# State products of units 2 and 3 in four 64x64 tiles, with two steps of the opening moved

## The chip, the cores and the metric

The kernel runs on one core of a Trainium2 chip. The metric is the device time of one execution in microseconds, as the median of several runs. All times below are microseconds unless marked ns. The engines are TensorE (in the profile PE for its matmuls, PEld for its weight loads), VectorE (DVE), ScalarE (ACT), GpSimd (POOL) and SyncE (SP, which issues DMAs).

## The reference

A retention layer is followed by a feed-forward layer with a leaky ReLU whose slope differs by channel:

```python
for t in range(S):                       # q, k, v: 4 batches, 8 heads, 768 tokens, 64
    state = gamma * state + outer(k[t], v[t])      # gamma differs by head
    y[t] = scale * q[t] @ state
x = y.transpose(0, 2, 1, 3).reshape(3072, 512)
h = x @ w_in                             # 512 x 2048
g = maximum(h, 0) + alpha * minimum(h, 0)
out = g @ w_out                          # 2048 x 512, float32
```

## The kernel before, in words

**Tiling.** The 3072 tokens are 12 units of 256 (three units to a batch), and two units make a block of 512 for the feed-forward layer, six blocks in all. Inside a unit there are two chunks c of 128 tokens. The recurrence is computed by chunks: within a chunk as masked scores times v, and across chunks as the query times a 64x64 state per head, which is carried from chunk to chunk with a decay of gamma^128. Units 2 and 5 are the last of their batches; unit 3 begins a batch, so that it has a state for its second chunk only.

**Steps of a unit.** `rescale` multiplies k and q by powers of gamma, `turn_pe` transposes them on TensorE and ScalarE copies the result to `kq`, `score_mm` and `masks` make the masked scores, `sum_mm` makes the chunk sums of k times v. `state_sum` adds the carried state to a chunk's sum on VectorE (line 423) and multiplies by the decay (line 424, on the engine that the call names, V for VectorE and G for GpSimd). `state_copy` (lines 428 to 452) writes the float16 copy from which TensorE reads. `out_mm` (lines 492 to 543) makes y: state products first, then scores times v (line 533). `take_y` turns y into xT, the input of the feed-forward layer.

**Two layouts of the state.** Heads go in pairs p; a is the head's place in its pair. For units below SPLIT = 4 the states of a pair stand block-diagonally in a 128x128 tile (`tg`), and one matmul multiplies both heads' queries (line 501): four per chunk. For units from 4 on they stand as 64x64 tiles (`th`), with chunk c's states on partition half c, so that the four products of a pair (two chunks, two heads) use the four 64x64 quarters of the array (line 515): eight per chunk. Queries of head a stand on partition half a of `kq`. Where a differs from c, `move_q` (lines 207 to 220) copies them to the other half, in tile `qf`, and `state_copy` writes the half of the states that changes its partitions ("far") on ScalarE.

**Feed-forward.** `ffn1` is x times w_in with the leaky ReLU (ScalarE, then VectorE), `ffn2` the product with w_out for block 0; the later blocks use a seven-product scheme. w_out's 2048 rows are 16 groups of 128, called ft. Groups 0 to 7 are loaded early in float32 (`get_wo32`) and cast by GpSimd and VectorE (`cast_wo`, two groups a call). Groups 8 to 11 and 12 to 15 come by `get_wo(2)` and `get_wo(3)`, DMAs on GpSimd's queue that cast on the way (line 982).

**What sets the order.** The order on every engine is written out by hand: each engine works in the order in which the calls stand in the code. `ffn1` and `ffn2` are generators that stop after each matmul, and `tick(gen, m)` runs m more of them at that place. `ffn2(0, ..., parts=4)` (lines 800 to 824) goes through its 64 matmuls in this order: for each four of the ft, for each of four token quarters, those four ft. Between its ticks stand units 2 and 3's steps and the ticks of `half`, the first product of block 1. `held.append(get_wo(2))` makes the next query load on SyncE's queue wait for that DMA (`hold`, line 129).

**The opening.** Units 0 and 1 are prepared while w_in arrives in parts; each part is cast by GpSimd or ScalarE (`cast_wi`, lines 974 to 978). The first seven matmuls of block 0's first product read parts 0 and 1 and stand ahead of unit 1's output.

Of the kernel before, what the change touches and what calls it, by code (L numbers as in the profile page):

```python
# [22 lines left out]
def kernel(  # L23
# [20 lines left out]

    SPLIT = 4
    MID = 6
    U = 256
# [90 lines left out]
    def rows(x):  # L140
        return slice(64 * x, 64 * x + 64)
# [53 lines left out]
    def cast_v(eng, u, h0=0, h1=H):  # L195
        o = unit(u)[2][:, h0:h1].rearrange("p h r d -> p (h r d)")
        i = staged[u]["v"][:, h0:h1].rearrange("p h x -> p (h x)")
        if eng is nc.scalar:
            eng.activation(out=o, in_=i, func=COPY, bias=0.0, scale=1.0)
        else:  # L200
            eng.tensor_copy(out=o, in_=i)  # L201
# [2 lines left out]
        kdq, kq, _ = unit(u)  # L204
        nc.sync.dma_start_transpose(out=kq, in_=kdq.rearrange("p t r h d -> p (t r h d)"))

    def move_q(u, eng=None):

        _, kq, _ = unit(u)
        qf = sbp.tile([128, 2, NP, 64], F16, tag="qf", bufs=3, name=f"qf{u}")  # L210
        moved[u] = qf
        for c in range(2):
            o = qf[rows(c)]
            i = kq.rearrange("p (t r a) i -> p t r a i", t=2, r=2)[
                rows(1 - c), 1, :, :, rows(c)
            ]
            if eng is not None:
                eng.activation(out=o, in_=i, func=COPY, bias=0.0, scale=1.0)
            else:
                nc.sync.dma_start(out=o, in_=i)  # L220

    def turn_pe(u, hh, bank):

        kdq, kq, _ = unit(u)
        trb = ps(bank, "trb", F16, 1024)
        n = 0
        for t in range(2):
            for r in range(2):
                for p in (2 * hh, 2 * hh + 1):
                    nc.tensor.transpose(  # L230
                        out=trb[:, n : n + 128],
                        in_=kdq[:, t, r, 2 * p : 2 * p + 2, :].rearrange("p a d -> p (a d)"),
                        identity=ident,
                    )
                    n += 128
        nc.scalar.activation(  # L236
            out=kq.rearrange("p (x a) i -> p x a i", x=4)[:, :, 2 * hh : 2 * hh + 2, :],
            in_=trb.rearrange("p (x a i) -> p x a i", x=4, a=2),
            func=COPY,
            bias=0.0,  # L240
            scale=1.0,
        )
# [167 lines left out]
    def state(u, c, eng, copy="gg"):  # L410

        state_copy(state_sum(u, c, eng), copy)
# [15 lines left out]
    def state_copy(uct, copy="gg", part=None):  # L428

        if uct is None:  # L430
            return
        u, c, t = uct
        to = (u, 1) if c == 0 else (u + 1, 0)
        if to[0] >= SPLIT:
            tg = tgs.get(to) or tgs.get((to[0], 1 - to[1]))
            if tg is None:
                tg = sbp.tile([128, 2, NP, 64], F16, tag="th", bufs=3, name=f"th{to[0]}")
        else:
            tg = tgbuf[(2 * u + c) % len(tgbuf)]
        tgs[to] = tg  # L440
        for a in range(2):
            if copy[a] == "-":
                continue
            far = to[0] >= SPLIT and a != to[1]
            if part is not None and far != part:
                continue
            i = t[rows(a)]
            o = tg[rows(to[1]), a] if to[0] >= SPLIT else tg[rows(a), :, rows(a)]
            if far or copy[a] == "a":
                nc.scalar.activation(out=o, in_=i, func=COPY, bias=0.0, scale=1.0)  # L450
            else:
                nc.gpsimd.tensor_copy(out=o, in_=i)
# [39 lines left out]
    def out_mm(u, banks, evict=True):  # L492
        _, kq, vx = prepped[u]
        ys = [ps(banks[0], "y0"), ps(banks[1], "y1")]
        inter = [(u, c) in tgs for c in range(2)]
        assert inter == [u % UPB > 0, True]

        for c in range(2):
            for p in range(NP):
                if inter[c] and u < SPLIT:  # L500
                    nc.tensor.matmul(
                        out=ys[c][:, 128 * p : 128 * p + 128],
                        lhsT=tgs[u, c][:, p, :],
                        rhs=kq.rearrange("p (t r a) i -> p t r a i", t=2, r=2)[
                            :, 1, :, p, rows(c)
                        ],
                        start=(p == 0),
                        stop=False,
                        skip_group_check=True,
                    )  # L510
        for p in range(NP):
            for c in range(2):
                for a in range(2):
                    if inter[c] and u >= SPLIT:
                        nc.tensor.matmul(  # L515
                            out=ys[c][rows(a), 128 * p : 128 * p + 128],
                            lhsT=tgs[u, c][rows(c), a, p, :],
                            rhs=qmove(kq, a, c, p) if a == c else moved[u][rows(c), :, p, :],
                            start=(p == 0),
                            stop=False,  # L520
                            skip_group_check=True,
                        )
        for p in range(NP):
            m2s = live[u, p // 2]
            for r in range(2):
                for c in range(2):
                    for a in range(2):
                        o = ys[c][rows(a), 128 * p : 128 * p + 128]
                        at, n = 256 * r + 128 * (p % 2), 128
                        if u >= SPLIT and r == 1:  # L530
                            at, n = 256 + 64 * (p % 2), 64
                            o = o.rearrange("p (r i) -> p r i", r=2)[:, :, 32:64]
                        nc.tensor.matmul(  # L533
                            out=o,
                            lhsT=vx[rows(c), 2 * p + a, r, :],
                            rhs=m2s[a][rows(c), at : at + n],
                            start=(r == 0 and p == 0 and not inter[c]),
                            stop=(r == 1),
                            skip_group_check=True,
                        )  # L540
        live[u] = ys
        if evict:
            take_y(u, (0, 1))
# [20 lines left out]
    def w_sums(i, lo, hi, eng=nc.vector):  # L564

        w = w_out_all.rearrange("p (k f) (j e) -> p k f j e", k=2, j=2)
        w12, w21, w22 = w[:, 0, lo:hi, 1, :], w[:, 1, lo:hi, 0, :], w[:, 1, lo:hi, 1, :]
        t1, t2, t3, t4 = (wsum[:, x, lo:hi, :] for x in range(4))
        o, a, b = (
            (t1, w12, w[:, 0, lo:hi, 0, :]), (t2, w22, t1), (t3, w22, w12), (t4, w21, t2)  # L570
        )[i]
        return eng.tensor_tensor(out=o, in0=a, in1=b, op=SUB)  # L572
# [386 lines left out]
    def tick(gen, m=10**6):  # L959
        for _ in range(m):  # L960
            if next(gen, 1) == 1:
                return
# [11 lines left out]
    def cast_wi(eng, lo, hi):  # L974
        o, i = w_in_all[:, :, 128 * lo : 128 * hi], win_part(lo, hi)
        if eng is nc.scalar:
            return eng.activation(out=o, in_=i, func=COPY, bias=0.0, scale=1.0)
        return eng.tensor_copy(out=o, in_=i)  # L978
# [18 lines left out]
    V, G, A = nc.vector, nc.gpsimd, nc.scalar  # L997
# [63 lines left out]
    take_y(0, (1,), V)  # L1061
    cast_v(G, 1, 0, 4)
    cast_v(G, 1, 4, 8)
    state_copy(s01, "g-")
    cast_wi(G, 0, 1)
    score_mm(1, 0, (4, 5))
    masks(1, 0)
    turn_pe(1, 1, 1)
# [1 line left out]
    cast_wi(A, 1, 2)  # L1070
    keep(2, 0)
    sum_mm(1, (6, 7))
    state(1, 0, V, "ga")
    cast_wi(G, 2, 3)
    cast_wi(A, 3, 4)
    get_wi(12, 14)
# [7 lines left out]
    s11 = state_sum(1, 1, V)  # L1084
    gen = ffn1(0, (2, 3, 6, 7, 0, 1, 2, 3, 6, 7, 4, 5, 0, 1, 2, 3), apart=4)
    tick(gen, 7)
    cast_wi(G, 4, 6)
    cast_wi(G, 6, 8)
    state_copy(s11)
    get_wo32(2)  # L1090
    get_wo32(3)
    load(2, "v")
# [18 lines left out]

    gen = ffn2(0, (0, 1, 2, 3), parts=4)
    half = ffn1(1, (6, 7, 4, 5, 4, 6, 0, 1, 2, 3, 0, 4, 5, 6, 7, 1), apart=12)
    tick(gen, 8)
    turn_pe(2, 0, 5)
    tick(gen, 6)
# [2 lines left out]
    masks(2, 0)  # L1119
    wsum = sbp.tile([128, 4, HF, HM], F16, tag="wsum", name="wsum")  # L1120
    turn_pe(2, 1, 4)
    tick(gen, 5)
    score_mm(2, 1, (6, 7))
    sum_mm(2, (5, 4))
    state(2, 0, G, "ga")
    masks(2, 1)
    held.append(get_wo(2))
    load(4)
# [3 lines left out]
    get_wo(3)  # L1132
    cast_v(G, 3)
    w_sums(0, 0, HF, G)
    tick(gen, 7)
    out_mm(2, (4, 5))
    tick(gen, 6)
    tick(half, 24)
    turn_pe(3, 0, 6)
    tick(half, 8)  # L1140
    turn_pe(3, 1, 7)
    tick(half, 16)
    tick(gen, 9)
    score_mm(3, 0, (4, 5))
    masks(3, 0)
    sum_mm(3, (6, 7))
    state(3, 0, G, "ga")
    rescale(G, 4, 0, 0, 8)
    tick(gen, 8)
    score_mm(3, 1, (4, 5))  # L1150
# [25 lines left out]
    a, b = steps(6, 3, 5, 0, "p"), steps(4, 6, 2, 1, "v")  # L1176
# [11 lines left out]
    for n in range(1, NBLK):  # L1188
        more = n + 1 < NBLK
        u0 = 2 * (n + 1)  # L1190
        if n > 1:
            gen = begun
# [22 lines left out]
        if more and u0 >= MID:  # L1215
# [34 lines left out]
            s11 = behind_middle(m11)  # L1250
# [87 lines left out]
```

## Time and profile before

| | us |
|---|---|
| median of 3 runs (198.47 to 198.94) | 198.59 |
| the profiled execution, its own time | 198.86 |
| its span, first to last instruction | 196.9 |
| TensorE's matmuls busy | 189.3 (96%) |
| VectorE / ScalarE / GpSimd busy | 156.3 / 115.4 / 106.1 |

The profile is of one execution. A row of the timeline has the start and the length in microseconds, the engine, the line of the kernel, the operation, output tile <- inputs, shapes, and how many instructions of that kind are merged in it (x8); in brackets stands the idle time of the engine before them and what ended it. Matmuls are pipelined, so that the length of a merged row runs beyond the start of the next; what a step costs TensorE is read from start to start. A row of the stretches has, for each engine, its busy time and number of instructions, then the granted TensorE clock, the share of the DMA engines and GB/s.

### The profile page before, as it was taken

The page shows a single profiled execution, that of the slowest core. Times are in us where ns is not written, and L with a number is a line of the kernel's source. Part 1 is how long each engine was busy: PE and PEld are TensorE (multiplying, and loading weights), DVE is VectorE, ACT ScalarE, POOL GpSimd, SP SyncE. Part 2 cuts the span into 40 slices and gives each one's busy share as a digit, 9 for nine tenths or more (in the row PEclk, how much of TensorE's full clock was granted, in tenths as well). Part 3 has the DMA queues.
Part 4 walks back from the last instruction along what each step waited for, and adds up shares of the span by engine and source line. Part 5 has one row for each costly group of instructions (what it writes and reads, how often), then busy time and mean ns, then how long its engine had stood idle before and what let it go on. Part 6 is the DMA issues. An engine that isn't in the chain of part 4 may idle for free.

```text
span 196.9 us, 6085 instructions
## 1 busy us (share of the span) xinstructions
PE 189.3 (96%) x2529; PEld 128.8 (65%) x2529; DVE 156.3 (79%) x259; ACT 115.4 (59%) x199; POOL 106.1 (54%) x113
## 2 busy tenths in 40 slices
PE   6688999999999999999999999999999999999993
PEld 2356645568467688744688744788644788865882
DVE  7698987517698998289988389977489996999983
ACT  4458665349187668467467476467466486678110
POOL 3176897499549544970077980076970180039300
PEclk9999999999999999999999999999999999999998
DMA  5999999998879989898988899929865010400014
GB/s 156 313 317 380 374 381 377 293 180 136 211 192 200 286 197 265 213 311 175 213 203 209 256 201 191 222 65 225 256 122 126 17 57 3 160 3 0 0 65 152
DMA packets 90026, 37.92 MB, mean 193 GB/s; under 512 B 57984, under 2 KB 87696, under 8 KB 90000
## 3 DMA queue, kind: packets, MB, share of 16 engines
q1 hardware_dynamic: 88768, 36.45, 69.2%
q0 software_dynamic: 1056, 1.05, 3.6%
q8 instruction: 20, 0.33, 0.6%
q10 hardware_dynamic: 176, 0.04, 0.1%
q14 instruction: 6, 0.05, 0.1%
HBM read 27.31 MB, written 6.29 MB: 171 GB/s over the span
## 4 chain that ended last, share of the span: by engine, by line
PE 90%; SPq 4%; DMA 3%; DVE 0%; issue 0%; POOL 0%; DVEq 0%
PE hps L632 36%; PE ox L857 16%; PE oy L857 12%; PE ops L809 7%; SPq L165 4%; PE hps L719 4%; PE sp L761 3%; DMA vs<-in_v_dram 3%; PE y L533 1%; PE y L384 1%; PE trb L230 1%; PE st L284 1%; PE sca L466 1%; PE ov L857 1%; PE ow L857 1%; PE oz L857 1%
## 5 line engine op out<-in xcount | busy, mean ns | idle before, releaser
L632 PE MATMUL hps<-xT,win 128*128 128x512 f16 (+1 forms) x396 | 71.5, 338 | 0.3 <-DVE ss L423 0.3
L650 DVE SCALAR_TENSOR_TENSOR gt<-hm,oma,hps 128x512 f16<-128x512 f32 (+1 forms) x96 | 59.4, 656 | 12.1 <-issue 4.3
L648 ACT ACTIVATE hm<-hps 128x512 f32<-128x512 f32 x80 | 47.6, 597 | 24.6 <-PE hps L632 22.5
L632 PEld LDWEIGHTS <-win 128*128 128x128 f16 x396 | 38.1, 98 | 31.0 <-POOL win L978 0.4
L857 PEld LDWEIGHTS <-gs 128*128 128x128 f16 x320 | 31.0, 98 | 3.7
L857 PEld LDWEIGHTS <-gt 128*128 128x128 f16 x240 | 22.9, 98 | 4.0
L333 POOL CAST tg<-tm 64x256 f16<-64x256 f32 x12 | 4.8, 396 | 34.3 <-DVE tm L301 22.3
L185 POOL TENSOR_TENSOR kdq<-qs,tab 128x1024 f16<-128x1024 f32 (+1 forms) x12 | 20.2, 1686 | 3.0 <-DVE wsum L572 2.3
L185 POOL TENSOR_TENSOR kdq<-ks,tab 128x1024 f16<-128x1024 f32 (+1 forms) x12 | 20.2, 1686 | 2.6 <-PE y L515 2.6
L857 PE MATMUL ox<-wout,gt 128*128 128x256 f16 x144 | 17.3, 273 | 0.0
L857 PE MATMUL oy<-wsum,gs 128*128 128x256 f16 x144 | 17.2, 273 | 0.0
L556 ACT ACTIVATE xT<-y 128x512 f16<-128x512 f32 x22 | 14.9, 744 | 3.1 <-PE y L533 2.0
L201 POOL CAST vx<-vs 128x1024 f16<-128x1024 f32 (+1 forms) x13 | 12.6, 970 | 6.7 <-DMA vs<-in_v_dram 6.7
L809 PE MATMUL ops<-wout,gt 128*128 128x512 f16 x64 | 15.3, 380 | 0.0
L613 DVE TENSOR_TENSOR gs<-gt 128x1024 f16<-128x1024 f16 (+1 forms) x14 | 13.0, 934 | 0.2
L877 ACT ACTIVATE cu<-oy 128x512 f32<-128x512 f32 x10 | 6.0, 597 | 10.6 <-PE oy L857 10.1
L236 ACT ACTIVATE kq<-trb 128x1024 f16<-128x1024 f16 x8 | 8.2, 1023 | 6.3 <-PE trb L230 6.3
L313 POOL TENSOR_TENSOR tf<-ss,tab 128x256 f32<-128x256 f32 x10 | 10.3, 1028 | 2.5 <-DVE ss L312 1.3
L881 DVE TENSOR_TENSOR os<-ox,cu 128x512 f32<-128x512 f32 x5 | 3.4, 687 | 10.1 <-PE ox L857 10.1
L670 POOL TENSOR_SCALAR hn<-qc,oma 128x256 f32<-128x256 f32 x4 | 4.5, 1138 | 12.4 <-DVE qc L785 12.3
L809 PEld LDWEIGHTS <-gt 128*128 128x128 f16 x64 | 5.8, 98 | 6.0
L424 POOL TENSOR_TENSOR tf<-ss,tab 128x256 f32<-128x256 f32 x6 | 5.9, 980 | 7.1 <-DVE ss L423 7.1
(119 smaller groups left out, 293.1 us busy)
## 6 DMA issues: line engine op xcount, KB each, us to landing
qs<-in_q_dram SPq DMA_DIRECT2D x9, 512.0 KB, 5.4
ks<-in_k_dram SPq DMA_DIRECT2D x32, 128.0 KB, 3.5
vs<-in_v_dram SPq DMA_DIRECT2D x32, 128.0 KB, 4.6
early<-in_moe_w_in_dram SPq DMA_DIRECT2D x7, 512.0 KB, 7.5
out_dram<-os SPq DMA_DIRECT2D x9, 256.0 KB, 2.5
early<-in_moe_w_out_dram SPq DMA_DIRECT2D x4, 512.0 KB, 7.0
out_dram<-ot SPq DMA_DIRECT2D x4, 512.0 KB, 3.8
ks<-in_k_dram SPq DMA_DIRECT2D x6, 256.0 KB, 6.1
```

Of the source, the lines that this page charges most:

```text
L165: nc.sync.dma_start(out=t[nm[0]][:, h, :], in_=src[b, h, U * c : U * c + U, :].rearrange("h (p r) d -> p h (r d)", r=2),)
L185: return eng.tensor_tensor(out=kdq[:, t, :, h0:h1, :].rearrange("p r h d -> p h r d"), in0=staged[u]["kq"[t]][:, h0:h1, :].rearrange("p h ...
L201: eng.tensor_copy(out=o, in_=i)
L236: nc.scalar.activation(out=kq.rearrange("p (x a) i -> p x a i", x=4)[:, :, 2 * hh : 2 * hh + 2, :], in_=trb.rearrange("p (x a i) -> p x a ...
L313: nc.gpsimd.tensor_tensor(out=t, in0=ss, in1=dec, op=MULT)
L556: nc.scalar.activation(out=o, in_=i, func=COPY, bias=0.0, scale=1.0,)
L613: last_g.append(nc.vector.tensor_tensor(out=o, in0=a, in1=b, op=op))
L632: nc.tensor.matmul(out=hps[:, f, U * (ul - lo) : U * (uh - lo)].rearrange("p (u t) -> p u t", t=U), lhsT=w_in_all[:, hp, 128 * (f0 + f) : ...
L648: nc.scalar.activation(out=hm, in_=hps, func=RELU, bias=0.0, scale=-1.0)
L650: nc.vector.scalar_tensor_tensor(out=gt[:, f0 + f, U * lo : U * hi], in0=hm[:, f, :], scalar=oma_sb[:, f0 + f : f0 + f + 1], in1=hps[:, f, :],
L809: nc.tensor.matmul(out=opss[tq], lhsT=gt[:, ft, 128 * tq : 128 * tq + 128], rhs=w_out_all[:, ft, :], start=(ft == 0), stop=(ft == NFT - 1),)
L857: nc.tensor.matmul(out=o[1][m], lhsT=lhs(f, m), rhs=rhs(f), start=(first and f == 0 and (m == 0 or o[0] is None)), stop=(f == HF - 1), ski ...
```

## The change

A new limit `QUARTERS = 2` takes the place of `SPLIT` in `state_copy` and `out_mm`, so that units 2 and 3 also use the 64x64 tiles; their other steps keep the layout of before. Their queries are moved by ScalarE, for unit 3 those of the second chunk alone. The state that unit 1 hands to unit 2 is copied in two steps, the near half at the old place and the far half after block 0's first product. Around unit 2's output the ticks of `gen` are 8 and 7 instead of 7 and 6, and a later tick is 8 instead of 9. In the opening, the cast of w_in's part 0 goes ahead of a state copy on GpSimd, and the decay of unit 1's first state goes from VectorE to GpSimd.

```diff
+    QUARTERS = 2
     SPLIT = 4
...
-    def move_q(u, eng=None):
+    def move_q(u, eng=None, cs=(0, 1)):
...
-        for c in range(2):
+        for c in cs:
...
-        if to[0] >= SPLIT:
+        if to[0] >= QUARTERS:
...
-            far = to[0] >= SPLIT and a != to[1]
+            far = to[0] >= QUARTERS and a != to[1]
...
-            o = tg[rows(to[1]), a] if to[0] >= SPLIT else tg[rows(a), :, rows(a)]
+            o = tg[rows(to[1]), a] if to[0] >= QUARTERS else tg[rows(a), :, rows(a)]
...
-                if inter[c] and u < SPLIT:
+                if inter[c] and u < QUARTERS:
...
-                    if inter[c] and u >= SPLIT:
+                    if inter[c] and u >= QUARTERS:
...
+    cast_wi(G, 0, 1)
     state_copy(s01, "g-")
-    cast_wi(G, 0, 1)
     score_mm(1, 0, (4, 5))
...
-    state(1, 0, V, "ga")
+    state(1, 0, G, "ga")
...
-    state_copy(s11)
+    state_copy(s11, part=False)
...
     half = ffn1(1, (6, 7, 4, 5, 4, 6, 0, 1, 2, 3, 0, 4, 5, 6, 7, 1), apart=12)
+    state_copy(s11, part=True)
     tick(gen, 8)
...
     turn_pe(2, 1, 4)
+    move_q(2, A)
     tick(gen, 5)
...
-    state(2, 0, G, "ga")
+    state(2, 0, G)
     masks(2, 1)
     held.append(get_wo(2))
...
     w_sums(0, 0, HF, G)
+    tick(gen, 8)
+    out_mm(2, (4, 5))
     tick(gen, 7)
-    out_mm(2, (4, 5))
-    tick(gen, 6)
     tick(half, 24)
...
     tick(half, 16)
-    tick(gen, 9)
+    move_q(3, A, (1,))
+    tick(gen, 8)
     score_mm(3, 0, (4, 5))
     masks(3, 0)
     sum_mm(3, (6, 7))
-    state(3, 0, G, "ga")
+    state(3, 0, G)
```

## The prediction

> **What bounds the kernel now.** First the page: busy shares and the chain of waits.
>
> ```profile
> span 196.9 us, 6085 instructions
> PE 189.3 (96%) x2529; PEld 128.8 (65%) x2529; DVE 156.3 (79%) x259; ACT 115.4 (59%) x199; POOL 106.1 (54%) x113
> PE 90%; SPq 4%; DMA 3%; DVE 0%; issue 0%; POOL 0%; DVEq 0%
> ```
>
> TensorE is busy 96% of the span and carries 90% of the chain that ended last. After the opening the chain holds next to nothing else. So two things count: how long TensorE's instructions take, and any moment at which it stands still; nothing later has room to give a standstill back. Next I read TensorE's timeline around the touched units, because its matmul counts show how far the interleaved second product of block 0 (line 809, `gen`) has come at each point.
>
> ```profile
> 31.68 1.89 PE L809 MATMUL ops<-wout,gt 128*128 128x512 f16 x8
> ...
> 33.85 1.46 PE L809 MATMUL ops<-wout,gt 128*128 128x512 f16 x6
> ...
> 36.04 1.24 PE L809 MATMUL ops<-wout,gt 128*128 128x512 f16 x5
> ...
> 37.92 1.68 PE L809 MATMUL ops<-wout,gt 128*128 128x512 f16 x7
> 39.44 0.74 PE L501 MATMUL y<-kq,tg 128*128 128x128 f16 x8
> 40.11 0.64 PE L533 MATMUL y<-m,vx 64*64 64x128 f16 x32
> 40.68 1.47 PE L809 MATMUL ops<-wout,gt 128*128 128x512 f16 x6
> ...
> 48.46 2.11 PE L809 MATMUL ops<-wout,gt 128*128 128x512 f16 x9
> ...
> 55.17 0.38 PE L501 MATMUL y<-kq,tg 128*128 128x128 f16 x4
> ...
> 56.06 1.68 PE L809 MATMUL ops<-wout,gt 128*128 128x512 f16 x7
> ```
>
> The counts are the ticks: 8, 6, 5, 7, then unit 2's output (L501, L533), then 6. That is 32 by 42 us, and the 33rd comes only at 48.46. The generator with parts=4 runs four row groups of w_out (ft) for each of four token quarters, so every 16 matmuls it moves on by four groups. Exactly 32 use ft 0 to 7; the 33rd is the first to read ft 8. Those rows do not come by the early loads but by `get_wo(2)`, a DMA that GpSimd issues. So the third view is GpSimd's timeline, with what SyncE's queue waits for.
>
> ```profile
> 38.59 0.61 POOL L424 TENSOR_TENSOR tf<-ss,tab 128x256 f32<-128x256 f32 x1 [2.15 <-DVE ss L423]
> 39.27 0.39 POOL L452 CAST tg<-tf 64x256 f16<-64x256 f32 x1
> 39.61 0.99 POOL L982 DMA_DIRECT2D wout<-in_moe_w_out_dram  x1
> ```
> ```profile
> SPq L165 <- DMA wout<-in_moe_w_out_dram: 6.8, 1, 6.8
> ```
> ```profile
> 46.50 0.38 SPq L165 DMA_DIRECT2D qs<-in_q_dram  x1
> ```
> ```profile
> DMA to landing us min/median/max: 5.5/6.2/6.8
> ```
>
> `get_wo(2)` is issued at 39.61, behind the state's decay and copy of unit 2. The query load of unit 4 is made to wait for it (`hold`), waits 6.8 us and goes at 46.50. So ft 8 to 11 land at about 39.61 + 6.8 = 46.4. Before, TensorE needs them at 48.46, two microseconds later, and nobody notices.
>
> **The change, part by part.** *The moved ticks.* The diff makes 7 and 6 around unit 2's output into 8 and 7. Together with 8, 6 and 5 that is 34, so matmuls 33 and 34, which read ft 8 and 9, now stand ahead of the 24 `half` matmuls. (The tick of 9 becoming 8 brings the count to 42 again at the same later place.) When does TensorE get there? One L809 matmul costs (2.11 - 1.24)/4 = 0.217. From 37.92: eight are 1.74, unit 2's output is 0.91 (next part), five more are 1.09: 37.92 + 1.74 + 0.91 + 1.09 = 41.66. The data are there at 46.4. TensorE waits 46.4 - 41.65 = 4.75 us, and everything behind matmul 33 in its queue waits with it: the `half` matmuls, unit 3's transposes, and through them ScalarE's and VectorE's ReLU work. The issue cannot be earlier: GpSimd works in order, the decay ahead of it waits for VectorE's sum, which waits for TensorE's own products, and the diff leaves one near copy there as before. Any shift of the opening moves both ends alike. The nearest bound from below is the quicker landing of the two, 5.5 after issue, at 45.1: 3.45. I take 4.75, as its row is the same transfer at the same moment.
>
> *The clock behind such a stop.* Inside the span TensorE never stops that long, so the price is bounded by its two ends.
>
> ```profile
> 1.51 3.79 PE L106 MATMUL kps<-spin 128*128 128x512 f16 x10 [1.51 <-DVE spin L1004]
> ```
> ```profile
> 193.70:195.60 1.90, 0.00 (x0) 0.00 (x0) 0.41 (x1) 0.00 (x0) 0.00 (x0) 1.00 0.72 251
> 195.70:196.90 1.20, 0.00 (x0) 0.00 (x0) 0.00 (x0) 0.00 (x0) 0.00 (x0) 0.50 0.00 0
> ```
>
> In the table by stretches the column before the last two is the granted clock. After the last matmul it is still 1.00 until 195.6, and 0.50 from 195.7: less than two microseconds of rest halve it. The first row shows the way back: ten 512-wide matmuls on a rested TensorE take 3.79, where 10 x 0.217 and 0.16 for the last one's drain (2.11 - 9 x 0.217) would be 2.33. So one recovery costs 1.46. Bounds are 0 (the clock stays) and 2.9 (two such stretches until it rises). I take 1.46.
>
> *The four tiles of unit 2.* Eight matmuls of 128x128 become sixteen of 64x64, four of which (chunk c, head half a) work side by side. Units 4 and 5 already do this; unit 5 has the same neighbours, a 128-row product on either side:
>
> ```profile
> 75.49 1.91 PE L857 MATMUL oy<-wsum,gs 128*128 128x256 f16 x16
> ...
> 77.58 0.52 PE L533 MATMUL y<-m,vx 64*64 64x128 f16 x32
> ```
> ```profile
> 77.33 0.26 PEld L515 LDWEIGHTS <-th 64*64 64x64 f16 x16 [0.21 <-issue]
> ```
> ```profile
> L515 PEld LDWEIGHTS <-th x32: 102/106/107, 73.6 to 77.5; 64*64 64x64 f16 x32
> ```
>
> Sixteen 256-wide matmuls at half of 0.217 end their streaming at 77.24; the tiles start at 77.33, 0.09 later, and the next step at 77.58, so sixteen cost 0.25. Unit 2's L533 with its way out takes 40.68 - 40.11 = 0.57 and stays. New: 0.09 + 0.25 + 0.57 = 0.91. Old: 40.68 - 39.44 = 1.24, in which the second half of L501 also waited for the copy that ends at 39.66; one tick later it no longer does. Gain 0.33.
>
> The sixteen loads of unit 5 take 0.26 together, at 0.106 for one of them. [...]
>
> *Unit 3.* It has a state for the second chunk only: four matmuls become eight, and these use one half of the array rows, two side by side, so four rounds as in unit 5. Old: 56.06 - 55.17 = 0.89; new 0.09 + 0.25 + 0.57 = 0.91; +0.02, or down to -0.1 if the next product fills the idle half.
>
> *Queries and states on ScalarE.*
>
> ```profile
> L218 ACT ACTIVATE qf<-kq x4: 615/628/629, 68.7 to 73.2; 64x512 f16<-64x512 f16 x4
> ```
> ```profile
> 39.24 0.41 ACT L450 ACTIVATE tg<-tf 64x256 f16<-64x256 f32 x1 [1.97 <-POOL tf L424]
> ```
>
> Two query moves are 1.25 us behind unit 2's second transpose copy; ScalarE idles 1.97 before 39.24, so it is done by 38.6. Unit 3's one move and the far half of unit 1's last state (0.41) lie likewise in idle time, and its near half alone stays on GpSimd. Cost 0; without that cover the two moves would delay unit 2's output by up to 1.25, but the wait for ft 8 would swallow it.
>
> *The opening.*
>
> ```profile
> 15.72 0.61 POOL L978 CAST win<-early 128x512 f16<-128x512 f32 x1
> 16.86 0.39 POOL L452 CAST tg<-tf 64x256 f16<-64x256 f32 x1 [0.52 <-DVE tf L424]
> ```
> ```profile
> 16.16 0.63 ACT L977 ACTIVATE win<-early 128x512 f16<-128x512 f32 x1
> ```
> ```profile
> 16.37 0.42 DVE L424 TENSOR_TENSOR tf<-ss,tab 128x256 f32<-128x256 f32 x1
> ...
> 18.77 0.73 DVE L554 CAST xT<-y 128x512 f16<-128x512 f32 x1
> ```
> ```profile
> 16.39 0.96 PE L632 MATMUL hps<-xT,win 128*128 128x256 f16 x7 [0.29 <-DVE ss L423]
> 17.18 0.61 PE L501 MATMUL y<-kq,tg 128*128 128x128 f16 x8
> 17.72 0.74 PE L533 MATMUL y<-m,vx 64*64 64x128 f16 x32
> ```
> ```profile
> 18.39 0.88 PEld L632 LDWEIGHTS <-win 128*128 128x128 f16 x9
> 19.55 2.51 PEld L632 LDWEIGHTS <-win 128*128 128x128 f16 x21 [0.29 <-DVE xT L554]
> ```
> ```profile
> L424 POOL TENSOR_TENSOR tf<-ss,tab x6: 612/832/1529, 12.6 to 73.4; 128x256 f32<-128x256 f32 x6
> ```
>
> The cast of w_in part 0 ends at 16.33 and the seven matmuls start at 16.39. Moved ahead of a copy of 0.39, it ends some 0.3 earlier. But the fifth of the seven reads part 1, which ScalarE casts until 16.79, and now starts at 16.39 + 4 x 0.109 = 16.83. So the seven end where they do: 0. The decay leaves VectorE (0.42) for GpSimd, behind cast and copy, at about 16.45. GpSimd's six decays took 0.61 to 1.53. I take 0.61 (the row at 38.59, with mask products on VectorE as here): ready at 17.1, copied by 17.5, where the second half of L501 would start at 17.4. A wait of about 0.15. In return the masks come 0.4 earlier and the stall of L533 for them (0.67 for 17.72 to 18.39, where unit 2 needs 0.57) goes: 18.45 instead of 18.39. Behind it nine matmuls (0.98) run before xT is needed; now xT ends at 19.50, just after them, then at about 19.35. TensorE goes on at 19.45 instead of 19.55: -0.1, from -0.2 up to +0.8 with the decay at 1.53.
>
> **Sum.** -0.1 - 0.33 + 0.02 + 4.75 + 1.46 = +5.8. The profiled execution took 198.86 (its span 196.9 and 2.0 around it), 0.27 above the median of 198.59. So 198.86 + 5.8 = 204.66, and for the median 204.4.
>
> **The rivals.** *The rows are there in time.* If ft 8 had landed by 41.65 there would be no stop and no loss of clock: 198.59 - 0.41 = 198.2, no measurable change. It decides at a landing 2.0 us after issue; the shortest in the trace is 5.5, and nothing ahead of it on GpSimd gets shorter. 5%.
>
> *The clock stays up.* Then only the stop counts: 198.59 - 0.41 + 4.75 = 202.9. For it: the profile has one halving only, and that at the program's end. Against it: it has no rest of two microseconds that left the clock up. [...] 15%.
>
> *A shorter landing.* At 5.5 the stop is 3.45: 203.1. For it: the second such transfer. 15%.
>
> *The opening loses.* A decay of 1.53 on GpSimd adds 0.9: 205.3. 5%.
>
> **How the numbers follow.** The forecast has 60%: 204.4, by itself 203.6 to 205.8 (198.18 + 4.75 and a clock loss from half to twice 1.46). The range reaches down to a short landing with little clock lost (198.18 + 3.45 + 0.4 = 202.0) and up to 206.0. About 0.3%, 0.6 us, is what a measurement of this kernel tells from no change: only the first rival lies there or below. Faster 0.02, same 0.04, slower 0.94.
>
> **What would show it.** In the profile after: seven L809 matmuls behind unit 2's output of which the sixth starts late, a gap on TensorE from about 41.6 to 46.4 put down to the wout DMA; a granted clock of 0.50 near its end and matmuls of twice the duration for about three microseconds; L515 sixteen in 0.25 at 39.7; the ffn of block 0 restarting at about 19.45. No gap there, or one below 3 us, would make the prediction wrong.

## The result, and the profile after

The changed kernel takes 205.88 (median of 6 runs, 204.31 to 207.22) against 198.59 before (6 runs, 198.45 to 199.96): a ratio of 1.0359, 95% interval 1.0329 to 1.0389. The profiled execution took 204.31, the shortest of the six, with a span of 202.3. Ratios leave out runs that took over 1.5% longer than the fastest run of their kernel. In the changed kernel the lines stand one or more further down: 501 is 502, 515 is 516, 533 is 534, 809 is 810.

Busy shares, granted clock by slices, and the chain of waits of the page:

```profile
span 202.3 us, 6112 instructions
PE 190.3 (94%) x2541; PEld 129.0 (64%) x2541; DVE 156.1 (77%) x258; ACT 117.5 (58%) x203; POOL 106.2 (52%) x113
PEclk9999999976999999999999999999999999999999
PE 85%; DMA 6%; SPq 4%; ACT 1%; POOL 0%; issue 0%; DVE 0%; POOLq 0%
```

TensorE's busy time is nearly that of before (190.3 and 189.3), the span is 5.4 longer, and a DMA holds 6% of the chain where it held 3%. The clock dips in the ninth and tenth slice (0.7 and 0.6). TensorE's timeline around unit 2 shows the place:

```profile
36.74 1.90 PE L810 MATMUL ops<-wout,gt 128*128 128x512 f16 x8
...
38.57 0.24 PE L516 MATMUL y<-kq,th 64*64 64x128 f16 x1
...
38.82 0.62 PE L534 MATMUL y<-m,vx 64*64 64x128 f16 x32
39.37 1.25 PE L810 MATMUL ops<-wout,gt 128*128 128x512 f16 x5
45.88 1.01 PE L810 MATMUL ops<-wout,gt 128*128 128x512 f16 x2 [5.26 <-DMA wout<-in_moe_w_out_dram]
46.69 4.13 PE L633 MATMUL hps<-xT,win 128*128 128x256 f16 x24
```

Five of the seven matmuls behind unit 2's output run, then TensorE is idle for 5.26, put down to the w_out DMA, and matmuls 33 and 34 follow. The next matmul was due at 39.37 + 5 x 0.217 = 40.45 and began at 45.88: 5.43 lost. The chain over the same stretch goes through that transfer:

```profile
38.11 0.32 POOL th L453
38.43 7.41 DMA wout<-in_moe_w_out_dram
45.84 0.04 issue
45.88 1.01 PE ops L810 x2
```

In the table by stretches (busy time and instructions of PE, PEld, DVE, ACT and POOL; then the clock, DMA share and GB/s) the clock halves during the stop and stays so for 3.5 of work, 6.83 in all (42.61 to 49.44):

```profile
40.70:42.60 1.90, 0.00 (x0) 0.00 (x0) 0.00 (x0) 0.11 (x1) 1.90 (x2) 1.00 1.02 139
42.70:45.80 3.10, 0.00 (x0) 0.00 (x0) 0.00 (x0) 0.00 (x0) 3.10 (x4) 0.50 0.74 85
45.90:49.40 3.50, 3.50 (x15) 2.15 (x15) 0.00 (x0) 0.60 (x1) 3.17 (x1) 0.50 1.10 211
49.50:52.00 2.50, 2.50 (x28) 2.14 (x27) 2.26 (x6) 1.74 (x3) 0.00 (x0) 1.00 1.13 246
```

Every execution has its mean granted clock on record: 6.83 at 0.50 in a span of 202.3 makes the mean 0.983. Five of the six runs have 0.982 or 0.983, the sixth has 0.990; none kept the full clock.

All of this execution lies 1.2 earlier than that of before: 36.74 against 37.92, and 30.50 against 31.68 at the first eight ticks of `gen`. That is chance rather than the change. Over the profiles of all kernels in this document those eight ticks begin between 30.50 and 32.33 with the decay on GpSimd (ten profiles) and between 30.82 and 32.15 with it on VectorE (four). What moves the opening is not found. SyncE's issue of unit 1's first key load took 1.73 before and 0.64 after, but elsewhere the opening does not follow it (0.78 and 31.98, 1.45 and 30.92).

### The profile page after: what moved, and what is told of

The parts are those of the page before. It is cut to its first block, busy times and chain, and to the rows that moved or that the text cites. A ratio compares the mean times of both kernels' runs of the same rounds, so it can differ in the third digit from the quotient of the medians.

```text
span 202.3 us, 6112 instructions
## 1 busy us (share of the span) xinstructions
PE 190.3 (94%) x2541; PEld 129.0 (64%) x2541; DVE 156.1 (77%) x258; ACT 117.5 (58%) x203; POOL 106.2 (52%) x113
## 2 busy tenths in 40 slices
DMA packets 90026, 37.92 MB, mean 187 GB/s; under 512 B 57984, under 2 KB 87696, under 8 KB 90000
## 3 DMA queue, kind: packets, MB, share of 16 engines
q0 software_dynamic: 1056, 1.05, 3.7%
## 4 chain that ended last, share of the span: by engine, by line
PE 85%; DMA 6%; SPq 4%; ACT 1%; POOL 0%; issue 0%; DVE 0%; POOLq 0%
PE hps L633 35%; PE ox L858 16%; PE oy L858 12%; PE ops L810 5%; SPq L166 4%; DMA wout<-in_moe_w_out_dram 4%; PE hps L720 3%; PE sp L762 3%; DMA early<-in_moe_w_in_dram 3%; PE y L385 1%; PE trb L231 1%; PE st L285 1%; PE y L534 1%; PE ov L858 1%; PE y L399 1%; PE ow L858 1%
## 5 line engine op out<-in xcount | busy, mean ns | idle before, releaser
L633 PE MATMUL hps<-xT,win 128*128 128x512 f16 (+1 forms) x396 | 72.8, 343 | 0.2 <-ACT win L978 0.2
L633 PEld LDWEIGHTS <-win 128*128 128x128 f16 x396 | 38.8, 100 | 31.7 <-issue 0.8
L810 PE MATMUL ops<-wout,gt 128*128 128x512 f16 x64 | 15.9, 387 | 5.3 <-DMA wout<-in_moe_w_out_dram 5.3
L810 PEld LDWEIGHTS <-gt 128*128 128x128 f16 x64 | 5.8, 98 | 11.5 <-issue 5.5
L451 ACT ACTIVATE th<-tf 64x256 f16<-64x256 f32 x18 | 7.5, 415 | 7.3 <-DVE tf L421 2.4
L453 POOL CAST th<-tf 64x256 f16<-64x256 f32 x16 | 6.3, 393 | 10.1 <-DVE tf L421 9.2
L314 POOL TENSOR_TENSOR tf<-ss,tab 128x256 f32<-128x256 f32 x10 | 10.3, 1028 | 2.5 <-DVE ss L313 1.3
```

Source lines behind the costliest of these rows:

```text
L314: nc.gpsimd.tensor_tensor(out=t, in0=ss, in1=dec, op=MULT)
L633: nc.tensor.matmul(out=hps[:, f, U * (ul - lo) : U * (uh - lo)].rearrange("p (u t) -> p u t", t=U), lhsT=w_in_all[:, hp, 128 * (f0 + f) : ...
L810: nc.tensor.matmul(out=opss[tq], lhsT=gt[:, ft, 128 * tq : 128 * tq + 128], rhs=w_out_all[:, ft, :], start=(ft == 0), stop=(ft == NFT - 1),)
```

## The experiments

The theory: the loss is the stop of TensorE for ft 8 plus the slow clock behind it. The rivals: the tiles, moves or opening cost something themselves, and the clock has no part. Each ratio is against runs of the kernel before on the same chip.

**Ticks undone.**

```diff
-    tick(gen, 8)
+    tick(gen, 7)
     out_mm(2, (4, 5))
-    tick(gen, 7)
+    tick(gen, 6)
...
     move_q(3, A, (1,))
-    tick(gen, 8)
+    tick(gen, 9)
```

> The changed kernel with the ticks of before (7, 6 and 9). Theory (the whole loss is the stop for ft 8 and the clock behind it): 198.2, no gap on TensorE near 41 us. Rival (tiles, query moves or the opening cost something themselves): above 199.

Measured: 199.06 (12 runs), before 198.82, ratio 1.0008 (0.9982 to 1.0033), and no stop. The whole loss goes with three numbers. The gain that the theory gave to the rest, 0.4, is not there.

**Ticks alone**, in the kernel before:

```diff
-    tick(gen, 7)
+    tick(gen, 8)
     out_mm(2, (4, 5))
-    tick(gen, 6)
+    tick(gen, 7)
...
-    tick(gen, 9)
+    tick(gen, 8)
     score_mm(3, 0, (4, 5))
```

> The kernel before with the new ticks (8, 7 and 8) and nothing else. Theory: the same stop, begun 0.3 later since unit 2's output is the slower one; landing unchanged, so 205 to 206 as the changed kernel. Rival (the ticks do harm only together with the tiles): 198.6.

Measured: 205.05 (6 runs), ratio 1.0305 (1.0262 to 1.0348). The old layout stops at the same place:

```profile
46.03 0.59 PE L809 MATMUL ops<-wout,gt 128*128 128x512 f16 x2 [4.36 <-DMA wout<-in_moe_w_out_dram]
```

So the ticks do it by themselves; nothing of the tiles is needed.

**Up to the limit.** The changed kernel with ticks 8, 5 and 10:

```diff
     out_mm(2, (4, 5))
-    tick(gen, 7)
+    tick(gen, 5)
...
-    tick(gen, 8)
+    tick(gen, 10)
     score_mm(3, 0, (4, 5))
```

> The changed kernel with ticks 8, 5 and 10: 32 matmuls ahead of the block of half, none that reads ft 8. Theory: no stop, 198.2 or somewhat less, as unit 2's state copy is no longer waited for. Rival (one matmul more ahead of unit 2 is what costs): 205.

Measured: 199.14 (12 runs), ratio 1.0009 (0.9981 to 1.0038). No stop; again no gain. Its profile shows two small waits in the place of the expected gain:

```profile
41.57 2.78 PE L633 MATMUL hps<-xT,win 128*128 128x256 f16 x24 [0.24 <-ACT xT L557]
44.74 0.61 PE L231 MATMUL trb<-mi,kdq 128*128 128x128 f16 x8 [0.39 <-DVE gt L651]
```

The first: five ticks (1.1) no longer cover ScalarE's copies of y to xT. The second is followed up below.

**One past the limit.** Ticks 8, 6 and 9, so that one matmul reads ft 8:

```diff
     out_mm(2, (4, 5))
-    tick(gen, 7)
+    tick(gen, 6)
...
-    tick(gen, 8)
+    tick(gen, 9)
     score_mm(3, 0, (4, 5))
```

> The changed kernel with ticks 8, 6 and 9: 33 matmuls, one alone reads ft 8. Theory (a step, not a slope): the full stop, 205.9 within 0.7. Rival (each matmul past the limit costs its share): about 202.

Measured: 204.04 (6 runs), ratio 1.0250 (1.0209 to 1.0290). That is below the theory's 205.2 to 206.6 and 2 above the rival's 202, so the time alone decides for neither. The profile does: for the sake of one matmul TensorE waits until the transfer lands.

```profile
PE ops L810 <- DMA wout<-in_moe_w_out_dram: 4.1, 1, 4.1
```

The point of decision is the 33rd matmul, as predicted: 32 cost nothing, 33 cost 5. In this profile the DMA landed 6.2 behind its issue and the stop was shorter (TensorE due at 41.14, at work again at 45.38: 4.24), but the slow clock lasted longer:

```profile
45.40:51.30 5.90, 5.90 (x29) 4.03 (x29) 1.75 (x4) 1.37 (x3) 4.37 (x2) 0.50 1.10 214
51.40:54.00 2.60, 2.60 (x33) 2.40 (x31) 1.55 (x4) 2.55 (x4) 0.00 (x0) 1.00 1.08 218
```

The profiled execution (205.06) is the longest of the six. Four of the others have a mean clock of 0.992 (an estimate by the sum above: about half of the slow stretch of 6.83) and took 203.62 to 204.34, which accounts for part of the distance from the theory.

**Busy while waiting.** 22 matmuls on constant data, read by nobody, ahead of the 33rd:

```diff
     out_mm(2, (4, 5))
-    tick(gen, 7)
+    tick(gen, 5)
+    keep(22, 7)
+    tick(gen, 2)
     tick(half, 24)
```

> The changed kernel with 22 matmuls on constant data (4.8 us) between the 32nd and the 33rd, whose results nobody reads. Theory (the stop costs twice, once as a rest and once through the clock): the granted clock stays 1.00, the landing is where it was, so the time is the changed kernel's less 1.5 to 1.8, about 204.2. Rival (the slow clock is no part of the loss): 205.9 or more.

Measured: 203.67 (5 runs), ratio 1.0277 (1.0254 to 1.0299), against 1.0359 (1.0329 to 1.0389) of the changed kernel.

```profile
40.85 1.25 PE L810 MATMUL ops<-wout,gt 128*128 128x512 f16 x5
41.94 4.91 PE L107 MATMUL kps<-spin 128*128 128x512 f16 x22
47.19 0.59 PE L810 MATMUL ops<-wout,gt 128*128 128x512 f16 x2 [0.34 <-DMA wout<-in_moe_w_out_dram]
```
```profile
47.20:52.00 4.80, 4.39 (x41) 3.57 (x41) 2.20 (x6) 2.33 (x4) 3.36 (x1) 1.00 1.12 240
```

The useful work stops as long as before (41.93 to 47.19, 5.26), but the clock stays at 1.00. From matmul 33 to matmul 35 behind the block of `half` it takes 47.19 to 54.32, 7.13; the changed kernel took 45.88 to 54.26, 8.38. The clock's part is 1.25 in these profiles and 0.8% (1.6) between the two ratios, as the theory had it. All five executions have a mean clock of 0.998 to 1.000. It is a real second part of the loss.

**Rows earlier.** The DMA issued behind unit 2's cast of v:

```diff
     cast_v(G, 2)
+    held.append(get_wo(2))
...
     masks(2, 1)
-    held.append(get_wo(2))
```

> The changed kernel with the DMA of ft 8 to 11 issued right behind unit 2's cast of v, some 2 us earlier on GpSimd. Theory (the stop ends when that transfer lands, and the transfer follows its issue): the stop is 1.5 to 2 us shorter, the time 203 to 204.3. Rival (the transfer is held up by the other traffic, so its landing stays): 205.9.

Measured: 204.02 (6 runs, 201.60 to 205.49), ratio 1.0239 (1.0189 to 1.0290), inside the theory's range. In its profile the issue is at 36.66 and the landing at 45.00, 8.3 later:

```profile
36.66 1.00 POOL L983 DMA_DIRECT2D wout<-in_moe_w_out_dram  x1
```
```profile
PE ops L810 <- DMA wout<-in_moe_w_out_dram: 3.0, 1, 3.0
```

Counted from the first of the eight matmuls ahead of unit 2's output (38.14 here, 36.74 in the changed kernel) the issue came 3.2 earlier and the landing 2.2 earlier. The transfer follows its issue, and 0.9 of the head start is lost on the way (8.3 against 7.4). One transfer of each kernel cannot say whether other traffic took that 0.9.

```profile
42.00:45.00 3.00, 0.02 (x1) 0.00 (x0) 0.00 (x0) 0.20 (x1) 3.00 (x3) 1.00 0.82 166
45.00:50.00 5.00, 4.55 (x43) 3.73 (x43) 2.36 (x6) 2.49 (x4) 4.53 (x2) 1.00 1.06 202
```

TensorE lost 3.2 (41.84 to 45.04) and the clock did not drop. Of the six runs it stayed up in two, the profiled one (202.38) and the shortest (201.60). The four with a mean clock of 0.992 or 0.983 took 203.44 to 205.49.

**The parts without the ticks.** Opening alone, in the kernel before:

```diff
+    cast_wi(G, 0, 1)
     state_copy(s01, "g-")
-    cast_wi(G, 0, 1)
...
-    state(1, 0, V, "ga")
+    state(1, 0, G, "ga")
```

> The kernel before with the two steps of the opening alone (cast ahead of the copy, decay on GpSimd). Prediction's term: -0.1, so 198.5. Rival (the changed kernel's earlier opening, 1.2 us in its profile, comes from these steps): 197.4.

Measured: 199.03 (12 runs), before 198.40, ratio 1.0023 (1.0009 to 1.0038): 0.46 slower by the ratio, against both expectations.

Tiles alone, the changed kernel with the ticks of the first experiment and the opening of before:

> The changed kernel with the ticks and the opening of before: tiles, query moves and split state copies alone. Prediction's terms -0.33 and +0.02: 198.3, with unit 2's block from its first state product to the next ft product 0.9 to 1.05 against 1.24. Rival (column tiles load slower and lose): 199 or more.

Measured: 198.45 (12 runs), ratio 1.0002 (0.9990 to 1.0013). No loss, but the expected 0.9984 (0.31 of 198.59) lies just outside. In its profiled execution (202.19) a load of v came late (GpSimd's cast waited 1.82 for it), so its total says nothing. The block of unit 2 can be read behind that wait: 42.18 to 43.28, 1.10, better than 1.24 and short of the expected 0.9 to 1.05.

The decay alone, in the kernel before:

```diff
-    state(1, 0, V, "ga")
+    state(1, 0, G, "ga")
```

> The kernel before with the decay of unit 1's first state on GpSimd and nothing else. Theory (the decay costs, not the cast): VectorE's first ReLU step of block 1 begins 0.5 behind its input instead of 0.09, time 198.9 to 199.1 against 198.5. Rival (the moved cast costs): 198.5 and 0.09.

Measured: 199.05 (12 runs), before 198.70, ratio 1.0024 (1.0008 to 1.0041), as much as the whole opening. So the decay carries it, as far as runs on two chips compare. One trace of it lies 28 us further on:

```profile
45.38 0.61 PE L230 MATMUL trb<-mi,kdq 128*128 128x128 f16 x8 [0.40 <-DVE gt L650]
```

VectorE begins its first ReLU step of block 1 0.49 behind ScalarE's output (43.87 to 44.37), where the kernel before needs 0.09 (43.84 to 43.93), and unit 3's transposes wait 0.40 for the bank that this frees. The profile gives VectorE's rest there as "issue", a wait for nothing it shows. All eight profiles up to here with the decay on GpSimd have a delay of 0.48 to 0.51, the three with it on VectorE 0.09. With the decay gone, 51 VectorE instructions stand ahead of that step instead of 52.

The opening with one more VectorE instruction, which leaves the computation as it is:

```diff
     masks(2, 1)
+    V.memset(sbp.tile([128, 16], FP, tag="pad", name="pad"), 1.0)
     held.append(get_wo(2))
```

> The kernel with the opening alone, and one VectorE memset of a spare tile (16 columns, read by nobody) behind the masks of unit 2, where VectorE idles over 4 us. Theory A (a matter of the number of VectorE instructions): the delay is back at 0.09 and the time at 198.4 to 198.6. Theory B (the decay's engine matters itself): delay 0.5, 199.0.

Measured: 199.47 (12 runs, 198.30 to 200.70), ratio 1.0038 (1.0012 to 1.0064). In the profile theory A holds, VectorE goes on after 0.10 and the transposes do not wait:

```profile
38.85 0.07 DVE L1127 MEMSET pad<- 128x16 f32 x1
43.19 2.56 DVE L650 SCALAR_TENSOR_TENSOR gt<-hm,oma,hps 128x256 f16<-128x256 f32 x6 [4.27 <-issue]
```

But the timed runs did not get shorter. So the delay is not shown to be what the decay costs.

**Two engines for xT.** Ticks 8, 5 and 10, and:

```diff
-    out_mm(2, (4, 5))
+    out_mm(2, (4, 5), evict=False)
+    take_y(2, (0,))
+    take_y(2, (1,), V)
```

> The changed kernel with ticks 8, 5 and 10, and unit 2's output moved to xT by ScalarE and VectorE together, one chunk each. In the run with ticks 8, 5 and 10 TensorE still waited 0.2 to 0.4 for xT, and 0.4 for a bank that VectorE's first ReLU step of block 1 frees, which began 0.5 after its input instead of 0.09. Theory A (that delay hangs on the number of VectorE instructions ahead, which this kernel brings back to that of before): both waits go, 198.0 to 198.3. Theory B (it hangs on the decay's engine): the first wait alone goes, 198.6 to 198.8.

Measured: 198.79 (12 runs), before 198.70, ratio 1.0012 (0.9992 to 1.0033). Both waits are gone from the profile (delay 0.09), as theory A had it; the time is not 0.4 to 0.7 lower. The same with the opening of before:

> As the run with ticks 8, 5 and 10 and two engines for xT, but with the opening of before (decay on VectorE, cast behind the copy). Theory B: delay 0.09 and the best time, 198.0 to 198.2. Theory A: one VectorE instruction more than before stands ahead, so the delay may be there or not; with it 198.5.

Measured: 198.43 (12 runs), ratio 0.9993 (0.9968 to 1.0018), delay 0.09. This is the lowest ratio of all, and not distinguishable from the kernel before. No version was found that beats it beyond the measurement.

## Why the prediction was right, point by point

**The stop** was right in place, cause and order of size: the sixth of the seven matmuls waits for `get_wo(2)`. Its size is 5.43 in the profile against 4.75. The arrival came out as worked out (2.0 behind the issue, 40.45 against 38.43); the landing was 7.41 behind the issue instead of the 6.8 of the one trace. Over the profiles of the kernels that stop it was 6.2 to 8.3. The changed kernel's times spread over 2.9 (204.31 to 207.22), those of the kernel before over 1.5 to 2.3 in its four series; that the landing makes the difference is likely and not shown, as one execution of each kernel has a profile. That a shift of the opening moves both ends alike held exactly: the issue comes 1.69 behind the first matmul ahead of unit 2's output in the kernel before, in the changed kernel and in three of the runs that stop. So the query moves also cost nothing, although the profile names one as what GpSimd's decay waited for.

**The clock** was right: halved in the stop, about 1.25 lost (predicted 1.46). The lower bound occurred in the profile of the run with earlier rows: nothing lost behind a stop of 3.2. The upper, 2.9, was approached one past the limit, behind a stop of 4.24: with 6.0 of slow work, matmul 33 to the next one behind `half` took 9.26, where 7.13 less one matmul (0.22) is 6.91, so 2.35 were lost. In the run of the ticks alone, three executions with a mean clock of 0.992 took 204.02 to 204.72, and three with 0.983 took 205.37 to 206.08. In the changed kernel's profile the clock halved 1.99 after the last matmul's end (40.62 to 42.61).

**The tiles of unit 2**: predicted 0.91 for the block, measured 39.37 - (36.74 + 8 x 0.217) = 0.89. With the ticks of before it is 1.06 in the profile of that run, as the state copies are then still waited for; so about half of the 0.33 belongs to the moved tick. The sixteen weight loads again took 0.26 together (38.57 to 38.83), where sixteen of 0.106 one behind another would be 1.7 (an estimate): they ran side by side. A single one took 0.106 for 64 columns where a 128x128 load (L810) took 0.098 for 128.

**Unit 3**: predicted +0.02 with -0.1 as its lower end. It is the lower end: in the changed kernel's timeline the products of scores already run between those of the state,

```profile
60.77 0.24 PE L516 MATMUL y<-kq,th 64*64 64x128 f16 x1
60.79 0.24 PE L534 MATMUL y<-m,vx 64*64 64x128 f16 x2
...
61.55 0.82 PE L810 MATMUL ops<-wout,gt 128*128 128x512 f16 x3
```

and the block from 60.76 to 61.55 takes 0.79 against 0.89. That the products of scores used the idle half of the array is a reading of these times, in which the rows of L534 begin 0.03 behind the first of L516.

**The opening** is the step that failed: "-0.1, from -0.2 up to +0.8". Alone it costs 0.46 (0.18 to 0.75), inside the bounds and on the other side of zero. The gain was read from two waits of one execution, the stall of L533 (0.67 where 0.57 is its length) and the 0.29 for xT. In the three other profiles with the decay on VectorE (the ticks alone, the tiles alone and the last run) L533 takes 0.57 and TensorE does not wait for xT there: the old opening mostly had nothing to gain. The cast's 0 held: the seven matmuls begin earlier and then wait 0.17 for ScalarE's part in the changed kernel. The decay's duration held too (0.61 in the changed kernel). One cost that was missed is a wait that the trace of before did not have. The decay now stands in GpSimd's queue behind the cast of w_in's part 0, and where that part lands late, copy and decay wait with the cast, as in the profile of the run with two engines for xT and ticks 8, 5 and 10:

```profile
16.22 0.62 POOL L979 CAST win<-early 128x512 f16<-128x512 f32 x1 [1.42 <-DMA early<-in_moe_w_in_dram]
16.78 0.40 POOL L453 CAST tg<-tf 64x256 f16<-64x256 f32 x1
17.14 0.61 POOL L425 TENSOR_TENSOR tf<-ss,tab 128x256 f32<-128x256 f32 x1
17.82 0.39 POOL L453 CAST tg<-tf 64x256 f16<-64x256 f32 x1
```
```profile
17.86 0.87 PE L502 MATMUL y<-kq,tg 128*128 128x128 f16 x8
18.65 0.53 PE L534 MATMUL y<-m,vx 64*64 64x128 f16 x24
```

The state products take 18.65 - 17.86 = 0.79 there, where 0.54 is their length without a wait. Four of the ten profiles with the decay on GpSimd have this wait (0.70 to 0.79); six do not (0.54), and the opening alone and the decay alone are among the six. An estimate from these ten is 0.1 on average, so it is not the whole of the 0.46. The other candidate is VectorE's delay far behind, but taking it away did not shorten the timed runs. What the decay costs stays open.

**The sum.** Predicted +5.8, measured +7.3 in the medians. If the one profile is taken for typical, the stop gives 0.7 of the difference and the clock takes off 0.2. In the runs of single parts the opening came out 0.56 above its term and the tiles with their moves and copies (0.04 by the ratio, against -0.31) 0.35 above theirs. That is 1.4 of the 1.5, put together from different runs, while landing and clock vary by more than what is left; so close a fit is in part luck. Luck is also that the profiled execution came within 0.4 of the 204.66 forecast for it: it stopped 0.7 longer than forecast, and its opening lay 1.2 earlier. The gains of the tiles show in the blocks, 0.24 to 0.28 for units 2 and 3 together with the ticks of before and 0.45 in the changed kernel. Why the times of the versions without a stop do not show them is not settled.

The first rival (rows there in time) needed a landing 2.0 behind the issue; no profile here has one under 5.5. The rival with the clock up is what the run with earlier rows had in its profile; in none of the changed kernel's six runs did the clock stay up. The shorter landing did not occur in the changed kernel's profile.

## What to carry to other kernels

Where work is interleaved by hand, a count of ticks is also a date: before moving one, count which operand slice the last step will read, and compare its landing in the trace with the time at which TensorE will arrive. The slack can be large in a profile (two microseconds here) and still be spent by moving a single matmul ahead of other work, and the price is then what is left of a transfer (3.2 to 5.4 here), not a matmul. If such a wait cannot be avoided, keeping TensorE busy through it saved the second price here, the slow clock (1.25 in the profiles, 1.6 by the ratios). And a gain that rests on a wait in one execution should be looked for in a second before it is counted.

## What the runs showed of the hardware

In the changed kernel's trace the granted clock falls to 0.50 at 42.61, 1.99 after the last matmul's modelled end (40.62), and is back at 1.00 at 49.44, 3.56 after TensorE went on (45.88). In the kernel before it falls at 195.64, again 1.99 after that end (193.65). The length of a rest alone does not decide: in the run with earlier rows a rest of 3.0 left the clock at 1.00. With the ticks alone it was still 1.00 behind the whole rest of 4.36 and fell between 46.9 and 47.0, though TensorE had been at work again for 0.9 to 1.0:

```profile
46.10:46.90 0.80, 0.80 (x6) 0.52 (x6) 0.00 (x0) 0.00 (x0) 0.80 (x1) 1.00 0.87 99
47.00:50.40 3.40, 3.40 (x18) 2.42 (x16) 1.04 (x3) 1.19 (x2) 2.85 (x1) 0.50 1.10 220
```

There it was back between 50.4 and 50.5, 3.4 to 3.6 later. One past the limit it fell between 44.5 and 44.6, inside the rest, and was back between 51.3 and 51.4, so that the slow work lasted 6.0. What decides when the clock falls and how long it stays down is not shown. What a stop lost by the slow clock differed from trace to trace: nothing behind a rest of 3.0, 1.25 behind 5.26, 2.35 behind 4.1.

In the kernels that stop, GpSimd's DMA of ft 8 to 11 (512 KB) landed 6.2 to 8.3 behind its issue, and the one issued earliest (36.66, the run with earlier rows) took longest, 8.3.

VectorE began one instruction 0.48 to 0.51 behind its input in the eight profiles in which 51 VectorE instructions stood ahead of it, and 0.09 or 0.10 in the six with 52 or 53, whether the one more was the decay, an unrelated memset or a copy to xT. The cause was not found.
